# Attention and two MoE layers on one core: the first sub-chunk of the second batch multiplied in float32 itself, not in split float32r words

## The chip, the cores and the metric

The kernel runs on one core of one Trainium2 chip. The metric is the device time of one execution in microseconds (us), as the median of several runs. An instruction belongs to one of five engines: TensorE (PE, its weight loads PEld), VectorE (DVE), ScalarE (ACT), GpSimd (POOL) and SyncE (SP, which here issues nearly all DMAs). Each engine runs its own instructions in the order in which they were built; waits between engines are semaphores.

## What is computed

```python
# q, k, v: (4 batches, 8 heads, 576 positions, 64), float32
scores = q @ k^T / 8;  rel = pos_q - pos_k
scores = where((rel >= 0) & (rel < 128), scores - slope[h] * |rel|, -1e9)
x = softmax(scores) @ v                   # heads side by side: (2304, 512)
h = max(x @ w1, x @ w2, x @ w3)           # each 512 x 768
y = h @ w_out                             # 768 x 512
g, val = y @ w_gate, y @ w_val            # each 512 x 1536
out = (g * sigmoid(g) * val) @ w_out2     # 1536 x 512
```

All is float32 and has to come out close to float32. In most products the kernel splits a number into a word rounded to float32r and the rest ("high" and "low"), and adds three float32r products (high-high, high-low, low-high).

## The kernel before, in words

**Sub-chunks, pairs, units.** A batch's 576 positions are two sub-chunks (`SUBS`): s = 0 with 256 positions, s = 1 with 320. A sub-chunk has four pairs of heads p, and a pair has a unit for each block of 128 positions: two units for s = 0, three for s = 1. A unit looks at its own 128 keys and at the 128 before them; the first unit of a batch (`k0` = 128) only at its own.

**A unit** goes through four steps. `st_scores`: scores into PSUM (`sc`), the mask (L299), the bias with the row's minimum (L304), exponential on ACT. `st_normalise`: reciprocal of the sums and a scaling. `st_transpose`: two transposes into the only `pt` buffer, a copy into SBUF, and two `affine_select` on POOL that make the masked halves `t`. `st_values`: the product with v into `pv`, then `split_x` on POOL, which writes the high and low words of x.

**Two ways to multiply.** Batch 0 is `native`: `load_first` brings, for each pair, the keys of both heads as 128 rows, and a query array `q0`/`q1` in which each head's 64 rows stand beside 64 rows of zeros. One float32 product over 128 rows then gives one head's scores (L291), and values are plain float32 products (L366). All other batches are split. `load_pair` brings each head by itself (`qk0`, `qk1`: q and k side by side, written twice, on partitions 0 to 63 and 64 to 127). `prep_head` makes `r` (ACT, L256), `kl` (DVE, through the helper at L77) and the low half of `r` (POOL, L77); `prep_v` makes v's high (ACT, L265) and low words (POOL, L77). Scores are two float32r products a head (L295, L296); `st_transpose` makes a low word of the transposed weights too (DVE, L77: `t` in a first unit, `pk` otherwise); `st_values` multiplies with v's two words (L374) and adds up three parts (L378 on ACT, L379 and two L381 on DVE).

**The buffers.** `qkr` has two buffers of 128 x 832, `rv` has two. In the split way both are free as soon as the prep has read them.

**Weights.** The first layer's 18 weight tiles w_f_e come from `words` (512 KB each) and are made in `prep_w`: ACT (L90), three DVE instructions (L93, L94, L96), a rounding cast on ACT (L99), the low word on DVE (L77). `mm3` multiplies: L111 and L112 need the high word, L113 the low one.

**The order.** `spread` lays the lists of work into one another: attention of sub-chunk 0 of batch 0 with the first weights; sub-chunk 1 with the rest and with `up_groups(0, 0)` (first layer on x of sub-chunk 0, called x_329 below); the attention of batch 1, sub-chunk 0, beside `up_groups(0, 1)` (x_611) and after. `prep_next` and `load_next` run one and two pairs ahead. A scheduler then moves instructions within each engine's list by its own forecast, so the order in which they stand is a result of the build.

Of the kernel before, what the change touches and what calls it, by code (L numbers as in the profile page):

```python
# [8 lines left out]
F32 = mybir.dt.float32  # L9
# [7 lines left out]
B, H, S, D = 4, 8, 576, 64  # L17
# [3 lines left out]
P = 128  # L21
NP = H // 2
KD = DM // P
NF1, NF2 = F1 // P, F2 // P
SUBS = ((0, 256), (256, 320))
KEY0 = (0, 128)
KEYN = (256, 512)
# [23 lines left out]
def kernel(ctx: ExitStack, tc, q0, k0, q1, k1, qk0, qk1, vv, w123, wo1, wgv, wo2, out):  # L51
# [10 lines left out]
    nc = tc.nc  # L62
# [131 lines left out]
    qkr = ea("qkr", 2)  # L194
# [16 lines left out]
    def load_first(s, p):  # L211

        nq, nk = SUBS[s][1], KEYN[s]
        c0, nkb = KEY0[s] // P, nk // P
        q = hp.tile([P, 2, nq], F32, tag=f"h{s}", name="qz", bufs=NF1)
        if s == 0:
            if p % 2 == 0:
                first["k", p] = first["k", p + 1] = qkr.tile([P, 832], F32, tag="qkr", name="kn")
                first["v", p] = first["v", p + 1] = vp.tile([P, 2, 2, 2, P], F32, tag="v", name="vn", bufs=3)
            k, v = first["k", p][:, p % 2 * nk:], first["v", p][:, p % 2, 0]  # L220
        else:
            k = prep.tile([P, 832], F32, tag="r", name="kn")
            if p % 2:
                v = vp.tile([P, 4, P], F32, tag="rv", name="vn")
            else:
                v = vp.tile([P, 4, 2, P], F32, tag="v", name="vn", bufs=3)[:, :, 0]
        nc.sync.dma_start(out=k[:, :nk], in_=(k0, k1)[s][p])
        nc.sync.dma_start(out=q, in_=(q0, q1)[s][p])
        if s == 0 and p % 2 == 0:
            nc.sync.dma_start(out=first["v", p][:, :, 0], in_=vv[0, p:p + 2, :, c0:c0 + nkb].rearrange("b p k d -> p b k d"))  # L230
        elif s:
            nc.sync.dma_start(out=v[:, :nkb], in_=vv[0, p, :, c0:c0 + nkb])
        return [q, k], v

    def load_pair(b, s, p):
        n = SUBS[s][1] + KEYN[s]
        c0, nkb = KEY0[s] // P, KEYN[s] // P
        heads = []
        for a in range(2):
            raw = qkr.tile([P, 832], F32, tag="qkr", name="qkr")  # L240
            nc.sync.dma_start(out=raw[:, :n], in_=(qk0, qk1)[s][b, 2 * p + a])
            heads.append(raw)
        v = vp.tile([P, 4, P], F32, tag="rv", name="rv")
        nc.sync.dma_start(out=v[:, :nkb, :], in_=vv[b, p, :, c0:c0 + nkb, :])
        return heads, v

    def native(b):


        return b == 0  # L250

    def prep_head(s, raw):
        nq, nk = SUBS[s][1], KEYN[s]
        r = prep.tile([P, 832], F32R, tag="r", name="r")
        kl = prep.tile([P, 512], F32R, tag="kl", name="kl")
        nc.scalar.copy(r[:, :nq + nk], raw[:, :nq + nk])  # L256
        low(nc.vector, kl[:, :nk], raw[:, nq:nq + nk], r[:, nq:nq + nk])
        low(nc.gpsimd, r[D:P, :nq], raw[D:P, :nq], r[D:P, :nq])
        return r, kl

    def prep_v(s, rv):
        nkb = KEYN[s] // P
        v = vp.tile([P, 4, 2, P], F32R, tag="v", name="v", bufs=3)
        rvv = rv.rearrange("p k (a d) -> p k a d", a=2)
        nc.scalar.copy(v[:, :nkb, :, 0:D], rvv[:, :nkb])  # L265
        low(nc.gpsimd, v[:, :nkb, :, D:P], rvv[:, :nkb], v[:, :nkb, :, 0:D])
        return v
# [11 lines left out]
    pairs = {}  # L279

    def st_scores(u):
        nq = SUBS[u.s][1]
        sc = ps_s.tile([P, 2, 256], F32, tag="sc", name="sc")
        c0 = nq + u.kb * P + u.k0
        c1 = nq + u.kb * P + 256
        m = u.mq
        for a in range(2):
            o = sc[:m, a, u.k0:]
            if native(u.b):
                qz, kn = pairs[u.b, u.s, u.p][:2]  # L290
                nc.tensor.matmul(o, qz[:, a, u.q0:u.q0 + m], kn[:, c0 - nq:c1 - nq], start=True, stop=True)  # L291
                continue
            r, kl = pairs[u.b, u.s, u.p][a]
            q = r[:, u.q0:u.q0 + m]
            nc.tensor.matmul(o, q, r[:, c0:c1], start=True, stop=False)  # L295
            nc.tensor.matmul(o, q, kl[:, c0 - nq:c1 - nq], start=False, stop=True)  # L296

        own = sc[:m, :, P:]
        nc.vector.copy_predicated(out=own, mask=later[:m], data=fill[:m].to_broadcast([m, 2, P]) if u.k0 else sc[:m, :, :P])  # L299
        z = u.z = zp.tile([P, 2, P], F32, tag="z", name="z")  # L300
        mn = small.tile([P, 2], F32, tag="mn", name="mn")
        sm = u.sm = small.tile([P, 2], F32, tag="sm", name="sm")
        for a in range(2):
            nc.vector.tensor_tensor_reduce(  # L304
                out=z[:m, a], in0=own[:, a], in1=bias[:m, 2 * u.p + a],
                op0=ALU.add, op1=ALU.min, scale=-0.125, scalar=3.0e38, accum_out=mn[:m, a:a + 1],
            )
        for a in range(2):
            nc.scalar.activation(  # L309
                out=z[:m, a], in_=z[:m, a], func=AF.Exp, scale=-1.0,  # L310
                bias=mn[:m, a:a + 1], accum_out=sm[:m, a:a + 1],
            )
# [16 lines left out]
    def st_transpose(u):  # L329

        m = u.mq
        plain = native(u.b)
        n, dt = (1, F32) if plain else (2, F32R)
        pt = ps_t.tile([P, 2, P], F32, tag="pt", name="pt")
        for a in range(2):
            nc.tensor.transpose(pt[:, a, :m], u.z[:m, a], ident[:m, :m])  # L336
        if u.k0 and not plain:
            t = u.t = ptp.tile([P, 2, 2, 2, P], F32R, tag="t", name="t")
            nc.scalar.copy(t[:, 1, 0, :, :m], pt[:, :, :m])
            low(nc.vector, t[:, 1, 1, :, :m], pt[:, :, :m], t[:, 1, 0, :, :m])  # L340
            return
        if u.k0:
            t = u.t = ptp.tile([P, 2, 2, 2, P], F32, tag="t", name="tn")
            nc.scalar.copy(t[:, 1, 0, :, :m], pt[:, :, :m])
            return
        w = ptp.tile([P, 2, 2, P], F32, tag="pk", name="pk")
        t = u.t = ptp.tile([P, 2, 2, 2, P], dt, tag="t", name="t")
        nc.scalar.copy(w[:, 0, :, :m].bitcast(dt), pt[:, :, :m])
        if not plain:
            low(nc.vector, w[:, 1, :, :m], pt[:, :, :m], w[:, 0, :, :m])  # L350
        for i, (op, sign) in enumerate(((ALU.is_gt, 1), (ALU.is_ge, -1))):
            nc.gpsimd.affine_select(  # L352
                out=t[:, i, :n, :, :m], in_=w[:, :n, :, :m], compare_op=op, fill=0.0, base=0,
                pattern=[[0, n], [0, 2], [-sign, m]], channel_multiplier=sign,
            )

    def st_values(u):
        m = u.mq
        i0 = u.k0 // P
        v = pairs[u.b, u.s, u.p][2]  # L360
        pv = ps_v.tile([P, 2, 2, P], F32, tag="pv", name="pv")
        xr = small.tile([P, P], F32, tag="xr", name="xr")
        if native(u.b):
            for a in range(2):
                for i in range(i0, 2):
                    nc.tensor.matmul(  # L366
                        pv[a * D:a * D + D, 0, 0, :m], v[:, u.kb + i, a * D:a * D + D], u.t[:, i, 0, a, :m],
                        start=i == i0, stop=i == 1,
                    )
            nc.scalar.copy(xr[:, :m], pv[:, 0, 0, :m])  # L370
            return split_x(u, xr)
        for a in range(2):
            for i in range(i0, 2):
                nc.tensor.matmul(  # L374
                    pv[:, a, :, :m], v[:, u.kb + i, a, :], u.t[:, i, :, a, :m], start=i == i0, stop=i == 1
                )
        c = small.tile([D, 2, P], F32, tag="c", name="c")
        nc.scalar.copy(c[:, :, :m], pv[D:P, :, 0, :m])  # L378
        nc.vector.tensor_tensor(out=c[:, :, :m], in0=pv[0:D, :, 1, :m], in1=c[:, :, :m], op=ALU.add)  # L379
        for a in range(2):  # L380
            nc.vector.tensor_tensor(  # L381
                out=xr[a * D:a * D + D, :m], in0=pv[0:D, a, 0, :m], in1=c[:, a, :m], op=ALU.add
            )
        split_x(u, xr)
# [24 lines left out]
    def prep_next(i):  # L409
        if i < len(todo):  # L410
            heads, rv = raws.pop(todo[i])
            b, s, p = todo[i]
            pairs[b, s, p] = heads if native(b) else [prep_head(s, r) for r in heads]
            pairs[b, s, p].append(rv if native(b) else prep_v(s, rv))

    def begin():

# [15 lines left out]
    for t in range(len(units) + LV):  # L433
        if t >= LV:
            u = units[t - LV]
# [7 lines left out]
        if t < len(units):  # L443
            u = units[t]
# [208 lines left out]
```

## Time and profile before

| | us |
|---|---|
| median of 3 runs (lowest, highest) | 912.55 (912.53, 913.21) |
| the profiled execution, its own time | 910.81 |
| its span, from the first to the last instruction | 909.1 |

| engine | PE | PEld | DVE | ACT | POOL |
|---|---|---|---|---|---|
| busy us | 879.1 | 783.6 | 490.9 | 353.0 | 414.1 |
| share of the span | 97% | 86% | 54% | 39% | 46% |

The page cuts the span into 40 slices of 22.7 us. In the first five the busy digit of DVE is 7, 8, 9, 9, 8 and that of PE 8, 8, 9, 6, 8; from the sixth slice on PE is at 9 in nearly all. A share of busy time is an average over stages with different limits, so the views below are taken by stretches of the span. The spans of matmuls overlap and their ends are modelled; DVE and ACT instructions in a row overlap by a little too (some 0.08 us).

### The profile page before, as it was taken

Reading aid. Unit: us, or ns where it says so; the run is one execution under the profiler, and the core shown is the slowest. Engines: PE = TensorE matmul, PEld = TensorE weight load, DVE = VectorE, ACT = ScalarE, POOL = GpSimd, SP = SyncE. Lnnn points to the kernel's source line nnn. Section 1 sums busy time; section 2 is a strip of 40 time slices with the busy share of each in tenths; the row PEclk is TensorE's granted clock in tenths of the full one; section 3 lists DMA queues with packets and bytes.
Section 4 is the critical chain, followed back from the end, with each engine's and each line's share of the span. In section 5 each row is a group of like instructions: output and inputs, shape, how many; then the busy total and the mean of one; then the engine's idle time right before and its main releaser. Section 6 shows DMA issues by size and latency. Waiting matters only on the chain.

```text
span 909.1 us, 14915 instructions
## 1 busy us (share of the span) xinstructions
PE 879.1 (97%) x5256; PEld 783.6 (86%) x5256; DVE 490.9 (54%) x1373; ACT 353.0 (39%) x988; POOL 414.1 (46%) x599
## 2 busy tenths in 40 slices
PE   8896899999999999999998999999999999999998
PEld 6675899999999999999976788888888888888897
DVE  7899987867677686647989941111111111111121
ACT  6887647756576566513444411000010001000101
POOL 5897557676777677542325522222222122221222
PEclk9997899999999999999998999999999999999999
DMA  9755224324232430125655533000210002000100
GB/s 334 256 151 168 86 70 122 115 73 141 67 111 59 131 109 28 44 83 174 220 203 170 182 93 123 17 1 0 93 47 1 1 1 93 1 1 0 47 1 23
DMA packets 40873, 82.74 MB, mean 91 GB/s; under 512 B 3680, under 2 KB 16480, under 8 KB 40800
## 3 DMA queue, kind: packets, MB, share of 16 engines
q1 hardware_dynamic: 39712, 79.71, 27.2%
q10 hardware_dynamic: 1088, 2.10, 0.7%
q8 instruction: 41, 0.67, 0.3%
q14 instruction: 32, 0.26, 0.1%
HBM read 67.63 MB, written 14.16 MB: 90 GB/s over the span
## 4 chain that ended last, share of the span: by engine, by line
PE 75%; issue 8%; DVE 7%; POOL 6%; DMA 2%; ACT 1%; ACTq 0%; SPq 0%; POOLq 0%; DVEq 0%
PE pg L113 9%; PE pg L111 9%; PE pg L112 9%; PE ps L111 9%; PE ps L112 9%; PE ps L113 9%; PE po L533 5%; PE po L531 5%; PE po L532 5%; PE pv L374 3%; POOL a L80 2%; PE pt L336 2%; DVE wf L94 1%; POOL a L77 1%; PE sc L296 1%
## 5 line engine op out<-in xcount | busy, mean ns | idle before, releaser
L80 POOL TENSOR_SCALAR a<-sg 128x512 fp32r<-128x512 f32 (+1 forms) x60 | 48.6, 810 | 330.7 <-DVE sg L518 327.3
L111 PE MATMUL pg<-y,u 128*128 128x512 f32 (+1 forms) x480 | 176.9, 369 | 1.2 <-DVE y L77 1.2
L113 PE MATMUL pg<-y,u 128*128 128x512 f32 (+1 forms) x480 | 176.8, 368 | 0.0
L112 PE MATMUL pg<-y,u 128*128 128x512 f32 (+1 forms) x480 | 176.8, 368 | 0.0
L111 PE MATMUL ps<-x,w 128*128 128x320 f32 (+1 forms) x576 | 173.3, 304 | 2.7 <-POOL x L80 1.5
L113 PE MATMUL ps<-x,w 128*128 128x256 f32 (+1 forms) x576 | 174.4, 304 | 1.3 <-DVE w L77 1.3
L112 PE MATMUL ps<-x,w 128*128 128x320 f32 (+1 forms) x576 | 173.6, 302 | 0.0
L517 DVE TENSOR_TENSOR sg<-pg,sg 128x512 f32<-128x512 f32 (+1 forms) x60 | 38.2, 637 | 249.7 <-ACT sg L516 249.7
L516 ACT ACTIVATE sg<-pg 128x512 f32<-128x512 f32 (+1 forms) x60 | 33.4, 556 | 317.2 <-PE pg L113 313.7
L111 PEld LDWEIGHTS ps<-x,w 128*128 128x128 f32 x576 | 110.5, 193 | 5.1 <-POOL x L80 2.1
L113 PEld LDWEIGHTS ps<-x,w 128*128 128x128 f32 x576 | 110.9, 193 | 3.3 <-DVE w L77 2.3
L112 PEld LDWEIGHTS ps<-x,w 128*128 128x128 f32 x576 | 110.9, 193 | 0.5 <-POOL x L80 0.2
L111 PEld LDWEIGHTS pg<-y,u 128*128 128x128 f32 x480 | 90.8, 189 | 17.0 <-DVE y L77 1.6
L112 PEld LDWEIGHTS pg<-y,u 128*128 128x128 f32 x480 | 90.6, 189 | 15.6
L113 PEld LDWEIGHTS pg<-y,u 128*128 128x128 f32 x480 | 90.6, 189 | 15.1
L352 POOL TENSOR_SCALAR_AFFINE_SELECT t<-pk 128x512 fp32r<-128x512 f32 (+3 forms) x128 | 72.9, 592 | 42.6 <-PE pv L374 20.5
L531 PE MATMUL po<-u,a 128*128 128x512 f32 x216 | 85.1, 394 | 2.2 <-POOL a L80 2.2
L533 PE MATMUL po<-u,a 128*128 128x512 f32 x216 | 84.9, 395 | 2.3 <-POOL a L77 2.3
L532 PE MATMUL po<-u,a 128*128 128x512 f32 x216 | 84.9, 393 | 0.0
L309 ACT ACTIVATE z<-z,mn 128x128 f32<-128x128 f32 (+1 forms) x160 | 63.4, 398 | 30.9 <-DVE mn L304 29.6
L77 POOL TENSOR_TENSOR a<-sg,a 128x512 fp32r<-128x512 f32 (+1 forms) x60 | 73.1, 1218 | 5.0
L518 DVE TENSOR_TENSOR sg<-pg,sg 128x512 f32<-128x512 f32 (+1 forms) x60 | 38.2, 637 | 58.5 <-PE pg L113 58.3
(83 smaller groups left out, 1707.5 us busy)
## 6 DMA issues: line engine op xcount, KB each, us to landing
wr<-wgv SPq DMA_DIRECT2D x24, 512.0 KB, 4.2
qkr<-qk SPq DMA_DIRECT2D x24, 416.0 KB, 3.5
wr<-w SPq DMA_DIRECT2D x18, 512.0 KB, 5.5
qkr<-qk SPq DMA_DIRECT2D x24, 256.0 KB, 2.8
wr<-wo SPq DMA_DIRECT2D x12, 512.0 KB, 4.7
y<-y_dram SPq DMA_DIRECT2D x12, 512.0 KB, 5.0
y_dram<-y SPq DMA_DIRECT2D x16, 320.0 KB, 2.6
out<-ob SPq DMA_DIRECT2D x18, 256.0 KB, 2.0
```

Source lines behind the costliest of these rows:

```text
L77: eng.tensor_tensor(out=out, in0=raw, in1=head.bitcast(F32), op=ALU.subtract)
L80: nc.gpsimd.tensor_scalar(out=out, in0=in_, scalar1=1.0, scalar2=1.0, op0=ALU.mult, op1=ALU.mult)
L111: nc.tensor.matmul(ps, wh, xt_h, start=first, stop=False)
L112: nc.tensor.matmul(ps, wh, xt_l, start=False, stop=False)
L113: nc.tensor.matmul(ps, wl, xt_h, start=False, stop=last)
L309: nc.scalar.activation(out=z[:m, a], in_=z[:m, a], func=AF.Exp, scale=-1.0, bias=mn[:m, a:a + 1], accum_out=sm[:m, a:a + 1],)
L352: nc.gpsimd.affine_select(out=t[:, i, :n, :, :m], in_=w[:, :n, :, :m], compare_op=op, fill=0.0, base=0, pattern=[[0, n], [0, 2], [-sign, m ...
L517: nc.vector.tensor_tensor(out=sg, in0=pair[0], in1=sg, op=ALU.mult)
L518: nc.vector.tensor_tensor(out=sg, in0=pair[1], in1=sg, op=ALU.mult)
L531: nc.tensor.matmul(po, ah, w2[f, 2][:, 0, :], start=f == 0, stop=False)
L532: nc.tensor.matmul(po, ah, w2[f, 2][:, 1, :], start=False, stop=False)
L533: nc.tensor.matmul(po, al, w2[f, 2][:, 0, :], start=False, stop=f == NF2 - 1)
```

## The change

Batch 1, sub-chunk 0 becomes `native` as well: 4 pairs, 8 units. The test takes (b, s), and the host lays out `q0` and `k0` for two batches.

```diff
+        if native(b, s):
+            raw = qkr.tile([P, 832], F32, tag="qkr", name="qkn")
+            nq, nk = SUBS[s][1], KEYN[s]
+            q, k = raw[:, :2 * nq].rearrange("p (a n) -> p a n", a=2), raw[:, 2 * nq:2 * nq + nk]
+            nc.sync.dma_start(out=k, in_=(k0, k1)[s][b, p])
+            nc.sync.dma_start(out=q, in_=(q0, q1)[s][b, p])
+            heads = [q, k]
-        for a in range(2):
+        for a in range(0 if heads else 2):
...
-    def native(b):
-        return b == 0
+    def native(b, s):
+        return b == 0 or (b, s) == (1, 0)
...
-            pairs[b, s, p] = heads if native(b) else [prep_head(s, r) for r in heads]
-            pairs[b, s, p].append(rv if native(b) else prep_v(s, rv))
+            pairs[b, s, p] = heads if native(b, s) else [prep_head(s, r) for r in heads]
+            pairs[b, s, p].append(rv if native(b, s) else prep_v(s, rv))
```

A pair now takes one `qkr` buffer in place of two, and holds it until its last scores; its `rv` buffer is held until its last values. With the lines moved, L295/L296 read L302/L303 in the new program, L291 reads L298, L366 reads L373, L374 reads L381, L299 reads L306, L304 reads L311, L316 and L318 read L323 and L325, L336 reads L343; L77 to L120 stay. A load of `load_pair` reads L243, L244 (keys, queries), L248 (a split head) and L251 (v).

**PE, where the fifth of six weight groups is multiplied** (`sc` scores, `pt` transposes, `pv` values, `ps` the layer's sums). Before:

```order
L295 MATMUL sc<-r 128x128
L296 MATMUL sc<-kl,r 128x128
L295 MATMUL sc<-r 128x128
L296 MATMUL sc<-kl,r 128x128
L111 MATMUL ps_1283<-x_329,w_4_2_1177 128x256
L112 MATMUL ps_1283<-x_329,w_4_2_1177 128x256
L336 MATMUL pt<-ident,z 128x128 x2
L374 MATMUL pv<-t,v 128x256 x2
L113 MATMUL ps_1283<-x_329,w_4_2_1177 128x256
```

Now:

```order
L298 MATMUL sc<-qkn 128x128 x2
L373 MATMUL pv<-tn,rv 64x128 x2
L343 MATMUL pt<-ident,z 128x128 x2
L111 MATMUL ps_1252<-x_329,w_4_2_1162 128x256
L112 MATMUL ps_1252<-x_329,w_4_2_1162 128x256
L298 MATMUL sc<-qkn 128x256 x2
L373 MATMUL pv<-t,rv 64x128 x4
L113 MATMUL ps_1252<-x_329,w_4_2_1162 128x256
```

At the same weight tile the new order has attention about one unit further on: the scores of the sub-chunk's last unit stand here, which stood after w_5_0's first products before.

**DVE, at the weights w_5_1**, the last but one of the first layer. Before:

```order
L77 TENSOR_TENSOR kl<-qkr,r 128x512
L96 SCALAR_TENSOR_TENSOR wr<-wr,wf 128x512
L77 TENSOR_TENSOR kl<-qkr,r 128x512
L77 TENSOR_TENSOR t<-pt,t 128x256
L77 TENSOR_TENSOR w_5_1_1302<-wr,w_5_1_1302 128x512
L93 TENSOR_SCALAR wf<-wf 128x256
L299 COPY_PREDICATED sc<-later,sc 128x2x128
L379 TENSOR_TENSOR c<-pv,c 64x256
```

Now:

```order
L94 SCALAR_TENSOR_TENSOR wf<-wr,wf 128x512
L77 TENSOR_TENSOR kl<-qkr,r 128x512
L325 RECIPROCAL rc<-sm 128x2
L96 SCALAR_TENSOR_TENSOR wr<-wr,wf 128x512
L77 TENSOR_TENSOR kl<-qkr,r 128x512
L77 TENSOR_TENSOR w_5_1_1271<-wr,w_5_1_1271 128x512
L93 TENSOR_SCALAR wf<-wf 128x256
L306 COPY_PREDICATED sc<-later,sc 128x2x128 x2
```

`t` (the low word of the transposed weights) and `c` (the adding up of values) are gone; the `kl` that remain are of the next sub-chunk, which is split still.

**SP, the loads around the last of the first layer's weights** (w123). Before:

```order
L241 DMA qkr_1408<-qk0 128x512
L241 DMA qkr_1410<-qk0 128x512
L120 DMA wr_1300<-w123 128x1024
L244 DMA rv_1220<-vv 128x256
L241 DMA qkr_1680<-qk1 128x832
L241 DMA qkr_1682<-qk1 128x832
L120 DMA wr_1367<-w123 128x1024
L244 DMA rv_1412<-vv 128x256
L244 DMA rv_1684<-vv 128x512
```

Now:

```order
L120 DMA wr_1269<-w123 128x1024
L120 DMA wr_1333<-w123 128x1024
L243 DMA qkn_1359<-k0 128x256
L244 DMA qkn_1359<-q0 128x512
L251 DMA rv_926<-vv 128x256
L248 DMA qkr_1607<-qk1 128x832
L248 DMA qkr_1609<-qk1 128x832
L251 DMA rv_1189<-vv 128x256
```

The last two w123 loads stand ahead of the last pair's loads. The two heads of the next sub-chunk (qkr_1607, qkr_1609) stand behind a v load and wait for PE's scores out of the same two buffers; their buffers waited for DVE's and POOL's prep before.

## Rows read from the trace of the kernel before

**Rows 1.** Busy time by stretch: length, then each engine (instructions), PEclk, DMA share, GB/s

```profile
40.00:102.00 62.00, 49.12 (x335) 40.77 (x334) 59.28 (x169) 49.59 (x156) 51.52 (x73) 0.86 0.46 138
...
55.00:102.00 47.00, 34.27 (x229) 29.52 (x229) 45.32 (x124) 36.34 (x111) 37.90 (x52) 0.82 0.47 140
102.00:105.60 3.60, 3.60 (x16) 3.60 (x15) 3.56 (x17) 1.67 (x7) 0.97 (x2) 0.53 0.52 179
105.60:400.00 294.40, 293.98 (x2261) 290.03 (x2261) 215.70 (x764) 178.90 (x564) 196.79 (x335) 1.00 0.28 86
```

**Rows 2.** What PE waited for, 0 to 105 us: total us, times, longest

```profile
PE pt L336 <- DVE t L77: 6.2, 2, 3.3
```

**Rows 3.** DVE by form, 40 to 102 us: busy us, mean ns | idle before

```profile
L94 DVE SCALAR_TENSOR_TENSOR wf<-wr,wf 128x512 int32<-128x512 int32 x12 | 10.3, 860 | 0.0
L96 DVE SCALAR_TENSOR_TENSOR wr<-wr,wf 128x512 int32<-128x512 int32 x12 | 9.6, 799 | 0.0
L77 DVE TENSOR_TENSOR w<-wr,w 128x512 fp32r<-128x512 f32 x12 | 9.1, 757 | 0.0
...
L304 DVE CUSTOM_DVE_ANT_0 z<-sc,bias 128x128 f32<-128x128 f32 x22 | 5.4, 280 | 1.6 <-PE pt L336 1.6
L77 DVE TENSOR_TENSOR kl<-qkr,r 128x512 fp32r<-128x512 f32 x4 | 4.3, 1064 | 0.0
...
L77 DVE TENSOR_TENSOR kl<-qkr,r 128x256 fp32r<-128x256 f32 x6 | 3.3, 561 | 0.0
...
L77 DVE TENSOR_TENSOR t<-pt,t 128x256 fp32r<-128x256 f32 x2 | 0.8, 409 | 0.0
L381 DVE TENSOR_TENSOR xr<-pv,c 64x128 f32<-64x128 f32 x2 | 0.6, 279 | 0.0
...
L77 DVE TENSOR_TENSOR pk<-pt,pk 128x256 f32<-128x256 f32 x1 | 0.4, 416 | 0.0
L379 DVE TENSOR_TENSOR c<-pv,c 64x256 f32<-64x256 f32 x1 | 0.4, 405 | 0.0
```

**Rows 4.** DVE in order of time: start, length, instruction

```profile
56.25 0.68 DVE L94 SCALAR_TENSOR_TENSOR wf<-wr,wf 128x512 int32<-128x512 int32 x1
...
67.90 1.22 DVE L94 SCALAR_TENSOR_TENSOR wf<-wr,wf 128x512 int32<-128x512 int32 x1
```

**Rows 5.** POOL in order of time, the same place

```profile
66.87 1.70 POOL L77 TENSOR_TENSOR r<-qkr,r 64x256 fp32r<-64x256 f32 x2
```

**Rows 6.** POOL by form, 40 to 102 us

```profile
L77 POOL TENSOR_TENSOR r<-qkr,r 64x256 fp32r<-64x256 f32 x7 | 6.0, 869 | 0.3
...
L77 POOL TENSOR_TENSOR v<-rv,v 128x256 fp32r<-128x256 f32 x4 | 4.1, 1025 | 0.0
```

**Rows 7.** PE in order of time: native scores and values of a unit, then split ones

```profile
47.93 1.03 PE L291 MATMUL sc<-kn,qz 128*128 128x256 f32 x4
49.13 0.66 PE L366 MATMUL pv<-t,vn 128*64 128x128 f32 x8
...
67.93 0.28 PE L295 MATMUL sc<-r 128*128 128x256 f32 x1
...
68.28 0.28 PE L296 MATMUL sc<-kl,r 128*128 128x256 f32 x1
...
96.43 0.71 PE L374 MATMUL pv<-t,v 128*128 128x256 f32 x4 [0.28 <-DVE xr L381]
```

**Rows 8.** DMA loads of the split way: KB each, median us from issue to landing

```profile
qkr<-qk SPq DMA_DIRECT2D x24, 416.0 KB, 3.5
...
rv<-vv SPq DMA_DIRECT2D x12, 256.0 KB, 2.7
```

**Rows 9.** Forms of the prep of s = 1, whole span: busy us, mean ns | idle before

```profile
L256 ACT CAST r<-qkr 128x832 fp32r<-128x832 f32 x24 | 20.2, 882 | 3.8 <-PE sc L296 3.5
...
L77 POOL TENSOR_TENSOR v<-rv,v 128x512 fp32r<-128x512 f32 x12 | 15.5, 1291 | 0.3
...
L265 ACT CAST v<-rv 128x512 fp32r<-128x512 f32 x12 | 7.4, 619 | 0.0
```

More of the change, by code (lines that the diff above doesn't have):

```diff
@@ L226, in load_first @@
                 v = vp.tile([P, 4, 2, P], F32, tag="v", name="vn", bufs=3)[:, :, 0]
-        nc.sync.dma_start(out=k[:, :nk], in_=(k0, k1)[s][p])
-        nc.sync.dma_start(out=q, in_=(q0, q1)[s][p])
+        nc.sync.dma_start(out=k[:, :nk], in_=(k0, k1)[s][0, p])
+        nc.sync.dma_start(out=q, in_=(q0, q1)[s][0, p])
         if s == 0 and p % 2 == 0:
@@ L288, in st_scores @@
             o = sc[:m, a, u.k0:]
-            if native(u.b):
+            if native(u.b, u.s):
                 qz, kn = pairs[u.b, u.s, u.p][:2]
@@ L331, in st_transpose @@
         m = u.mq
-        plain = native(u.b)
+        plain = native(u.b, u.s)
         n, dt = (1, F32) if plain else (2, F32R)
@@ L362, in st_values @@
         xr = small.tile([P, P], F32, tag="xr", name="xr")
-        if native(u.b):
+        if native(u.b, u.s):
             for a in range(2):
@@ L615, in apart @@
     def apart(x):
-        x = x[0].reshape(NP, 2, D, -1)
-        out = np.zeros((NP, 2, D, 2, x.shape[-1]), x.dtype)
+        x = x.reshape(-1, NP, 2, D, x.shape[-1])
+        out = np.zeros((len(x), NP, 2, D, 2, x.shape[-1]), x.dtype)
         for a in range(2):
-            out[:, a, :, a] = x[:, a]
-        return out.reshape(NP, P, 2, -1)
+            out[:, :, a, :, a] = x[:, :, a]
+        return out.reshape(len(x), NP, P, 2, -1)
     arrays = {
-        "q0": apart(qt[..., 0:256]),
-        "k0": c(kt[0, ..., 0:256].reshape(NP, P, 256)),
-        "q1": apart(qt[..., 256:576]),
-        "k1": c(kt[0, ..., 128:640].reshape(NP, P, 512)),
+        "q0": apart(qt[:2, ..., 0:256]),
+        "k0": c(kt[:2, ..., 0:256].reshape(2, NP, P, 256)),
+        "q1": apart(qt[:1, ..., 256:576]),
+        "k1": c(kt[:1, ..., 128:640].reshape(1, NP, P, 512)),
         "qk0": twice(np.concatenate([qt[..., 0:256], kt[..., 0:256]], axis=-1)),
```

## The prediction, made before the changed kernel ran

> **What bounds the kernel now.** I read the busy time by stretches first. From 105.6 to 400 us PE is busy 293.98 of 294.40 us at full clock: there the time is PE's work and nothing else. From 55 to 102 us it is otherwise: PE is busy 34.27 of 47.00 us, so 12.7 us idle, while DVE is busy 45.32 [rows 1]. What PE waited for, read next, names DVE as the largest releaser: two transposes waited 6.2 us for the low word `t`, because the only `pt` buffer is free only once DVE has read it [rows 2]. The forms on DVE then show what it does there: the four instructions of each weight tile, the attention units, and the `kl`, `t`, `pk`, `c` and `xr` of the split way. The one idle time among them is 1.6 us [rows 3]. So up to 102 us the kernel is bounded by DVE, and from there by PE. A gain has to come from the moment (call it M) at which PE reaches the first product of x_611, which is at 102 us; whatever makes M earlier, or leaves PE less to do behind M, moves everything that follows, since no stage behind it hangs on anything but the work before it.
>
> **The change, part by part.** The prep of 4 pairs goes: 8 `kl`, 8 low words of q on POOL, 4 of v on POOL, 12 casts on ACT. In the 8 units the low words `t`, `pk`, one `c` and two `xr` each go.
>
> *DVE up to M.* By the built order, what has left DVE ahead of M is: 8 `kl` of 256 columns, of which 6 lie in the stretch (3.3 us; the first two lie before 40 us, where DVE soon waits, and are counted at nothing), one of the 4 `kl` of 512 (1.06), two `t` (0.8), one `pk` (0.4), one `c` (0.4), two `xr` (0.6) [rows 3]. That is 6.5 us. What has come in ahead of M, because the order moved up: one more low word of a weight (0.76) and one more unit's two reductions (2 x 0.28) [rows 3], which I round up to 2.0 for that unit's reads, sum and reciprocal. Net: **-4.5**. The units of the sub-chunk that lie behind M lose their DVE work too, at no gain: PE is the bound there and covers it.
>
> *DVE beside POOL.* The same L94 on 512 columns takes 0.68 us at 56.25 and 1.22 us at 67.90 [rows 4]. At 67.90 POOL is in the middle of two low words of q, 66.87 to 68.57 [rows 5]; the L94 ended 0.55 us after them. So a DVE instruction can stand still while POOL works. Against 0.68 us the four 512-wide forms of the stretch lost 12 x (0.860 - 0.68) + 12 x (0.799 - 0.68) + 12 x (0.757 - 0.68) + 4 x (1.064 - 0.68) = 6.0 us [rows 3]. The change takes 6.0 + 4.1 = 10.1 us [rows 6] out of POOL's 51.5 us in the stretch [rows 1], a fifth. A fifth of 6.0 is 1.2; as other forms stretch too, I take **-2.0**, with ends 0 (other POOL work closes up into the room) and -10.1 (each removed POOL instruction had held DVE for its whole length). The Trainium skill, "SBUF — State Buffer", section "Who interferes with whom", says that a DVE instruction with two SBUF inputs contends with a GpSimd instruction that reads SBUF, and that the loser blocks until the other has ended. The 67.90 row agrees; by that rule alone this term would be at its far end and the sum below -15.8 in place of -7.7, which is the third rival.
>
> *PE.* A native unit's scores take 1.03 us for four records, a split unit's run from 67.93 to 68.56, 0.63 us: 0.4 more. The values are alike: 0.66 native, 0.71 split [rows 7]. The scores of a pair's first unit, on half the columns, I take as equal. Four such units make 4 x 0.4 = 1.6 us; all lie ahead of M in the new order and find 12.7 us of idle PE [rows 1]: **0**, and +1.6 if that cover is gone.
>
> *Work taken ahead of M.* In the new order ten products of x_329, four transposes, four products of scores and a unit's values stand ahead of the first x_611 that stood behind it before. A record of this size follows the last by 0.12 us (67.93, 68.28: three steps of 0.117) [rows 7], so about 20 of them are 2.4 us that PE no longer has to do behind M. PE must find that time ahead of M, from the same 12.7 us; it also waits in order there, so I take half: **-1.2** (ends 0 and -2.4). The granted clock was 0.82 in the stretch and 0.53 from 102 to 105.6, about half speed just as PE became the bound [rows 1]; 3.6 us at half speed cost 1.7. PE was idle before it; if its stalls go, the clock may stay up: I take half, **-0.8** (ends 0 and -1.7).
>
> *The loads.* A pair's two DMAs carry less than before. But the buffers are held longer. The two heads of the next sub-chunk now wait on SP for PE's scores out of the same buffers; they waited for prep, far ahead. Behind the last native scores there come the load, 3.5 us [rows 8], the cast on ACT, 0.88 [rows 9], and `kl` on DVE, 1.06 [rows 3]: 5.4 us until the second head can be multiplied. In between PE has about 30 records at 0.12, 3.8 us. Nothing else on SP suffers at once: the last two w123 loads stand ahead, and queued behind are only heads, v and w_out pieces. What waits is DVE (its `kl` stands ahead of w_5_1) and then PE. DVE has about 20 instructions of its own in between, so I take half of the missing 1.6: **+0.8** (ends 0 and +5.4). The v loads of the next sub-chunk wait likewise for native values, behind M, with some 10 us of PE work between: 0.
>
> The sum: -4.5 - 2.0 + 0 - 1.2 - 0.8 + 0.8 = -7.7 us against the profiled execution's own time of 910.81, that is 903.1. The median of the runs shown stands at 912.55, 1.74 above it; carried over, the forecast is **904.8 us**. With the ends of single terms together (-4.5 - 4.0 - 2.4 - 1.7) it goes to about 900, and with -4.5 + 1.6 and nothing else to 909.6.
>
> **The rivals.**
>
> *PE becomes the bound of the stretch.* DVE shrinks, but PE's products stand in a fixed order among waits for weights, transposes and POOL, and the float32 scores take 1.6 us more. If half of the 12.7 us idle stays, M comes 6.35 - 1.6 = 4.7 us earlier: 907.8. For it: the clock of 0.82 makes PE slow just there. Against: its longest waits were for DVE [rows 2].
>
> *Slower: the buffers of one pair.* Held until the scores and values, they turn loads that were far ahead into loads in the chain. If the heads of both the next pairs come bare (2 x 5.4) and one v load too (2.7 + 0.62 + 1.29 = 4.6) [rows 8, 9], PE and DVE stand 15.4 us. Without the +0.8 the gains are 8.5; so +6.9: 919.5. It decides from stalls of 8.5 us on. For it: the order on SP, and only two buffers. Against: 3.8 us of PE work and some 8 us of DVE work lie in between.
>
> *POOL had held DVE by the whole.* The mechanism of the 67.90 row for all 11 removed instructions: 10.1 in place of 2.0, so 8.1 us more: 896.7. The Trainium skill, by the rule cited above, would have it so. For it: that row. Against: POOL was busy 51.5 of 62 us and yet the four forms lost only 6.0 us in all.
>
> *No change in the time.* The next sub-chunk's prep, or the changed order further on, takes the time again before PE's long stretch begins: 912.5. Against: PE has nothing to wait for from 105.6 to 400 us.
>
> **How the numbers follow.** The forecast 0.60, PE as the bound 0.20, POOL by the whole 0.07, the buffers 0.07, no change 0.06. What a measurement of this kernel tells from no change is about 0.2%, 1.8 us. Faster by more than that are the forecast, the first and the third rival: 0.87; within it 0.06; slower 0.07. The range from 899.5 to 910.0 holds the forecast with its ends and the first rival, 0.80, and leaves out the other three.
>
> **What would show it.** Right: the first product of x_611 at 93 to 96 us instead of 102; no wait of a transpose for `t` before it; DVE still the busiest there, with shorter 512-wide forms; PE's busy time up by 1 to 2 us for the scores; the stretch behind M as dense as before. Wrong: a wait of DVE's `kl` or ACT's cast for a DMA ahead of w_5_1, PE waits of 3 us or more at the next sub-chunk's first scores or values, or M earlier while the end is not.

## The result, and the profile after

The changed kernel takes **904.35 us** (median of 4 runs, 903.22 to 905.86) against 912.88 (912.53 to 913.42) for the kernel before beside it: ratio 0.9906, 95% interval 0.9888 to 0.9924. The forecast was 904.8 in 899.5 to 910.0. Two later sessions, each beside the kernel before on the same chip, gave 0.9934 (0.9911 to 0.9958) and 0.9938 (0.9918 to 0.9957), so by the medians of the three sessions the gain is between 4.6 and 8.5 us, and the agreement to half a microsecond was closer than a session can tell. The profiled execution took 905.38 us (span 903.7) against 910.81: 5.4 us less.

Busy time by stretch in the changed kernel, to be read against [rows 1]; 94.3 us is where M now lies:

```profile
40.00:94.30 54.30, 47.02 (x353) 38.59 (x353) 52.28 (x170) 45.62 (x152) 41.64 (x60) 0.96 0.44 130
55.00:94.30 39.30, 32.95 (x249) 27.33 (x247) 38.73 (x123) 33.21 (x109) 29.81 (x41) 0.94 0.47 139
94.30:105.60 11.30, 11.30 (x74) 11.29 (x74) 9.30 (x29) 7.23 (x25) 4.59 (x10) 0.89 0.35 109
105.60:400.00 294.40, 294.40 (x2246) 286.97 (x2246) 200.70 (x717) 171.82 (x540) 193.41 (x332) 1.00 0.29 89
```

M, the first product on 320 columns, in PE's order of time, in the kernel before and then in the change:

```profile
101.76 0.31 PE L111 MATMUL ps<-x,w 128*128 128x320 f32 x1
```

```profile
94.30 0.47 PE L111 MATMUL ps<-x,w 128*128 128x320 f32 x1
```

What PE waited for up to 105 us in the change (total us, times, longest); the 6.2 us of [rows 2] for `t` are gone:

```profile
PE ps L113 <- DVE w L77: 3.2, 4, 1.5
PE sc L302 <- POOL r L77: 2.4, 1, 2.4
...
PE ps L111 <- POOL x L80: 1.5, 1, 1.5
```

DVE's forms from 40 to 94.3 us in the change, as in [rows 3]:

```profile
L77 DVE TENSOR_TENSOR w<-wr,w 128x512 fp32r<-128x512 f32 x13 | 10.2, 783 | 0.0
L96 DVE SCALAR_TENSOR_TENSOR wr<-wr,wf 128x512 int32<-128x512 int32 x12 | 10.0, 834 | 0.0
L94 DVE SCALAR_TENSOR_TENSOR wf<-wr,wf 128x512 int32<-128x512 int32 x12 | 8.7, 722 | 0.0
...
L77 DVE TENSOR_TENSOR kl<-qkr,r 128x512 fp32r<-128x512 f32 x3 | 2.9, 974 | 0.0
L323 DVE TENSOR_SCALAR sm<-sm 128x2 f32<-128x2 f32 x12 | 2.8, 232 | 0.0
```

So far the forecast's picture holds: DVE is still nearly full (38.73 of 39.30 us from 55 us to M), PE's idle time there fell from 12.7 us to 6.35, and M came 7.5 us earlier. DVE's busy time between 40 us and M fell from 59.28 us [rows 1] to 52.28, by 7.0 us. But of the 7.5 us the end kept only 5.4, although from 105.6 to 400 us PE shows no idle time at all. To see where the rest went, I took every record of PE from 12 us to the first gate product (`pg<-y,u`, at 452.09 us before and 447.98 after) and split that length into three: idle (no record under way), the price of the half-speed clock (half of the busy time that lies in stretches at 1.2 GHz), and PE's work, which is the rest. The busy time is in the first column behind the length, in the kernel before and then in the change:

```profile
12.00:452.09 440.09, 421.78 (x3124) 402.16 (x3123) 343.35 (x1117) 273.70 (x846) 289.96 (x468) 0.98 0.39 123
```

```profile
12.00:447.98 435.98, 422.78 (x3144) 399.34 (x3143) 326.02 (x1077) 268.33 (x833) 279.85 (x454) 0.99 0.39 124
```

| us | length | work | idle | half clock |
|---|---|---|---|---|
| before | 440.1 | 412.6 | 18.3 | 9.2 |
| change | 436.0 | 420.0 | 13.2 | 2.8 |
| change, last session (f1_change) | 436.7 | 420.3 | 11.7 | 4.8 |

Idle and half clock together fell by 11.5 us; PE's work rose by **7.4**. At the first gate product the change leads by 4.1 us; the other 1.3 us of the 5.4 come behind it, where the profile of the change has 1.0 us less idle and 1.2 us less half clock. Where the work rose is in PE's order of time behind M. In the kernel before, the split values stand among the other products (a product of 320 columns follows the last by 0.147 us):

```profile
126.96 0.31 PE L112 MATMUL ps<-x,w 128*128 128x320 f32 x1
127.10 0.28 PE L374 MATMUL pv<-t,v 128*128 128x256 f32 x1
127.22 0.31 PE L113 MATMUL ps<-x,w 128*128 128x320 f32 x1
127.36 0.52 PE L374 MATMUL pv<-t,v 128*128 128x256 f32 x3
127.73 0.38 PE L336 MATMUL pt<-ident,z 128*128 128x128 f32 x2
```

In the change the float32 values stand there, on 64 columns of weights (128*64):

```profile
124.37 0.31 PE L112 MATMUL ps<-x,w 128*128 128x320 f32 x1
124.61 0.43 PE L373 MATMUL pv<-tn,rv 128*64 128x128 f32 x2
124.97 0.41 PE L113 MATMUL ps<-x,w 128*128 128x320 f32 x1
125.31 0.43 PE L373 MATMUL pv<-tn,rv 128*64 128x128 f32 x2
125.67 0.41 PE L111 MATMUL ps<-x,w 128*128 128x320 f32 x1
125.93 0.30 PE L112 MATMUL ps<-x,w 128*128 128x320 f32 x1
```

Before, three records take 127.73 - 127.36 = 0.37 us, 0.12 each. In the change a run of two records (one float32 product shows as two) takes 124.97 - 124.37 - 0.147 = 0.45 us, the next two 125.67 - 124.97 - 0.147 = 0.55, with a gap on either side of the run (124.61 where 124.52 would do, 125.31 where 125.12 would). The gap behind a run is 125.93 - 125.67 - 0.147 = 0.10 us; with it a run of two costs 0.56. Behind M stand 32 of the 48 value records of the sub-chunk, in 12 runs: nine of two, two of four, one of six.

### The profile page after: what moved, and what is told of

Its sections match the earlier page's. It is cut to its first block, busy times and chain, and to the rows that moved or that the text cites. A ratio compares the mean times of both kernels' runs of the same rounds, so it can differ in the third digit from the quotient of the medians.

```text
span 903.7 us, 14864 instructions
## 1 busy us (share of the span) xinstructions
PE 879.6 (97%) x5280; PEld 779.8 (86%) x5280; DVE 470.9 (52%) x1333; ACT 347.5 (38%) x976; POOL 404.1 (45%) x587
## 4 chain that ended last, share of the span: by engine, by line
PE 82%; issue 6%; DVE 5%; POOL 5%; DMA 1%; ACT 1%; ACTq 0%; SPq 0%; DVEq 0%; POOLq 0%
PE pg L111 10%; PE pg L113 10%; PE pg L112 10%; PE ps L111 10%; PE ps L113 10%; PE ps L112 9%; PE po L540 5%; PE po L538 5%; PE po L539 5%; PE pv L381 2%; PE pt L343 2%; POOL a L80 1%; PE sc L303 1%; PE sc L302 1%; DVE wf L94 1%
## 5 line engine op out<-in xcount | busy, mean ns | idle before, releaser
L113 PE MATMUL ps<-x,w 128*128 128x256 f32 (+1 forms) x576 | 173.9, 303 | 3.2 <-DVE w L77 3.2
L111 PE MATMUL ps<-x,w 128*128 128x256 f32 (+1 forms) x576 | 173.4, 303 | 1.5 <-POOL x L80 1.5
L112 PE MATMUL ps<-x,w 128*128 128x256 f32 (+1 forms) x576 | 172.5, 300 | 0.0
L77 POOL TENSOR_TENSOR a<-sg,a 128x512 fp32r<-128x512 f32 (+1 forms) x60 | 72.7, 1211 | 5.0
L316 ACT ACTIVATE z<-z,mn 128x128 f32<-128x128 f32 (+1 forms) x160 | 63.3, 398 | 22.5 <-DVE mn L311 21.9
```

Of the source, the lines that this page charges most:

```text
L77: eng.tensor_tensor(out=out, in0=raw, in1=head.bitcast(F32), op=ALU.subtract)
L111: nc.tensor.matmul(ps, wh, xt_h, start=first, stop=False)
L112: nc.tensor.matmul(ps, wh, xt_l, start=False, stop=False)
L113: nc.tensor.matmul(ps, wl, xt_h, start=False, stop=last)
L316: nc.scalar.activation(out=z[:m, a], in_=z[:m, a], func=AF.Exp, scale=-1.0, bias=mn[:m, a:a + 1], accum_out=sm[:m, a:a + 1],)
```

## The experiments

My theory at this point: M comes earlier because DVE's prep ahead of it is gone; behind M some 4.5 us are given back, because each run of values on 64 columns costs PE some 0.3 us beyond its streaming, and no idle time shows it. The rivals: what is given back comes of the order; or float32 by itself is dear; or POOL, not DVE, had set M.

**e1_grouped, f2_grouped: the values of a unit behind one another**

```diff
+            with tc.high_priority(20000 if u.b else 0):
                 for a in range(2):
                     for i in range(i0, 2):
                         nc.tensor.matmul(
...
```

> The values of batch 1, sub-chunk 0 get a high priority, so that the two or four products of a unit stand behind one another on PE; nothing else is edited. Theory (each run of float32 values among float32r products costs PE some 0.3 us beyond its streaming, which no idle time shows): 32 records behind M stand in some 6 runs in place of 12 and cost about 4 us in place of 6.96; the time falls by 2 to 3.5 us, to 901 - 902.5. Rival 1 (what is given back behind M comes from the changed order of the products or from late work, not from the switch): within 1 us of 904.35. Rival 2 (a float32 record is dear by itself, whoever stands beside it): the cost per record stays at 0.22 us, 904 - 905.

Measured: 901.85 us, ratio to the kernel before 0.9861 (0.9838 to 0.9884). It was run once more beside the change:

> As e1_grouped. Theory (2.7 us of PE's work behind M were the price of standing singly): 0.3% below the changed kernel beside it, 0.1 to 0.5. Rival (the earlier 0.45% came from the chip and the throttle of that hour): within 0.1%.

Measured: 903.13, ratio 0.9904 (0.9881 to 0.9927) where the change beside it had 0.9938: 0.34% less, as the theory has it, though the intervals overlap. PE's order of time in e1_grouped:

```profile
105.31 0.31 PE L113 MATMUL ps<-x,w 128*128 128x320 f32 x1
105.55 0.66 PE L374 MATMUL pv<-t,rv 128*64 128x128 f32 x8
106.15 0.42 PE L111 MATMUL ps<-x,w 128*128 128x320 f32 x1
106.40 0.31 PE L112 MATMUL ps<-x,w 128*128 128x320 f32 x1
...
109.18 0.31 PE L113 MATMUL ps<-x,w 128*128 128x320 f32 x1
109.42 0.44 PE L374 MATMUL pv<-tn,rv 128*64 128x128 f32 x4
109.79 0.41 PE L111 MATMUL ps<-x,w 128*128 128x320 f32 x1
```

Four records take 0.46 us, eight 0.69: the time of a run, without the 0.10 behind it, goes 0.45, 0.46, 0.69 for 2, 4 and 8 records, so most of it is paid per run. The cost per record falls to 0.09 in the run of eight, which speaks against rival 2 of the expectation. In the change itself the runs of four and of six cost 0.78 each with the record behind them, so the count alone does not give the time. The 0.9861 of e1_grouped was measured without the change beside it.

**e2_fullcols, f3_fullcols: all 128 columns of weights**

```diff
+            wide = u.b == 1
             for a in range(2):
+                o, w = (pv[:, a, 0, :m], slice(0, P)) if wide else (pv[a * D:a * D + D, 0, 0, :m], slice(a * D, a * D + D))
                 for i in range(i0, 2):
...
+                    nc.tensor.matmul(o, v[:, u.kb + i, w], u.t[:, i, 0, a, :m], start=i == i0, stop=i == 1)
+            for a in range(2 if wide else 0):
+                h = slice(a * D, a * D + D)
+                nc.scalar.copy(xr[h, :m], pv[h, a, 0, :m])
...
```

> The native values of batch 1 take all 128 columns of v as the weights, each head into a part of its own of pv, and ACT copies the right half of each; so the float32 products keep the full array and give twice the output columns' work, of which half is thrown away. If the switch is dear because the values use 64 columns of the array: a run of two records behind M falls from 0.5 us to 0.25 - 0.3, the records take up to 0.05 us more each, the time falls by 1 to 3 us (901 - 903). If it is dear because of float32 beside float32r: runs of two stay at 0.5 or more, the time is 904 - 906. Rival 1 (order): no change, 904 - 905.

> As e2_fullcols. Theory (3.7 us of PE's work saved): 0.3 to 0.5% below the changed kernel beside it. Rival (chip and throttle): within 0.1%.

Measured: 902.82, ratio 0.9860 (0.9835 to 0.9885); then 901.91, ratio 0.9889 (0.9871 to 0.9908), 0.49% below the change beside it, whose interval lies wholly above. PE's order of time in e2_fullcols:

```profile
120.54 0.31 PE L112 MATMUL ps<-x,w 128*128 128x320 f32 x1
120.69 0.38 PE L375 MATMUL pv<-t,rv 128*128 128x128 f32 x2
120.83 0.40 PE L113 MATMUL ps<-x,w 128*128 128x320 f32 x1
121.06 0.83 PE L375 MATMUL pv<-t,rv 128*128 128x128 f32 x6
121.65 0.39 PE L111 MATMUL ps<-x,w 128*128 128x320 f32 x1
121.88 0.30 PE L112 MATMUL ps<-x,w 128*128 128x320 f32 x1
...
138.77 0.28 PE L112 MATMUL ps<-h,wo 128*128 128x256 f32 x1
138.89 1.05 PE L375 MATMUL pv<-t,rv 128*128 128x128 f32 x8
139.70 0.36 PE L113 MATMUL ps<-h,wo 128*128 128x256 f32 x1
139.90 0.28 PE L111 MATMUL ps<-h,wo 128*128 128x256 f32 x1
```

Two float32 records now take 120.83 - 120.54 - 0.147 = 0.14 us in place of 0.45. The record behind a run still starts late, by 121.06 - 120.83 - 0.147 = 0.08 us; with that two records cost 0.22 in place of 0.56. Six cost (121.65 - 121.06) + (121.88 - 121.65 - 0.147) = 0.67, and eight 0.81 + 0.08 = 0.89 (a product of 256 columns follows the last by 0.12). That is 0.11 a record in every run: the same data type, half of the output thrown away, and no price per run is left. So the 64 columns were dear in short runs, not float32. The order of cost turns with the length: a run of eight costs 0.69 + 0.10 = 0.79 us on 64 columns and 0.89 on 128. The Trainium skill, "TensorEngine Tiling (Array Packing)", section "Key Properties", says that a change of the tiling mode drains TensorE. By that rule every run on 64 columns pays on its way in and out, and the rows agree; here it was about 0.3 us for a run of two.

**e3_values_split, f4_values_split: only the scores native**

```diff
-        plain = native(u.b, u.s)
+        plain = u.b == 0
...
-        if native(u.b, u.s):
+        if u.b == 0:
...
-            pairs[b, s, p].append(rv if native(b, s) else prep_v(s, rv))
+            pairs[b, s, p].append(rv if b == 0 else prep_v(s, rv))
```

> Scores of batch 1, sub-chunk 0 stay native, its values go back to the split way (prep of v, low words t, c and xr return). Theory: DVE gets 2.2 us back ahead of M and POOL the 4 low words of v and the selections of two words, so M comes 2.2 to 4 us later than in the change (96.5 - 98.5); behind M nothing is given back (-4 to -5 against the change): in all 902 - 904.5, at or below the changed kernel. Rival 1 (what is given back behind M has nothing to do with the native values): M later and nothing won behind it, 906.5 - 908.5.

> As e3_values_split. Theory (the native values win some 2 us ahead of M and give back 3.1 us of PE's work, so the float32 scores alone carry the whole gain): within 0.2% of the changed kernel beside it. Rival (the native values do carry a gain of their own): slower than it by 0.2% or more.

Measured: 905.46, 1 us above what I expected, ratio 0.9901 (0.9881 to 0.9922); then 904.57, ratio 0.9925 (0.9908 to 0.9941), 0.13% below the change beside it. M came at 97.62 us in e3_values_split, 3.3 us later than in the first profile of the change. To compare what lies behind M I count the products `ps<-x,w` ("up products") from the start: M is the 197th in the kernel before and the 207th in the change, and the 217th lies behind M in both. From there to the first gate product the lead on the kernel before fell by 1.0 us only in e3_values_split (from 7.04 to 6.07), in the change from 9.28 to 4.11. PE's work in that stretch was 344.2 us, beside 344.4 in the kernel before and 348.9 in the change. Rival 1 falls by that: the order is much the same. At the 217th product e3_values_split was 2.2 us behind the change, and f4_values_split 1.8 us behind f1_change, with a like clock ahead of it in each of these pairs. So native values on 64 columns bring nothing that these runs can tell: they win some 2 us ahead of M and give them back behind it. The two intervals beside one another overlap.

**e4_scores_split: only the values native**

```diff
-        if native(b, s):
+        if b == 0:
...
-            if native(u.b, u.s):
+            if u.b == 0:
...
-            pairs[b, s, p] = heads if native(b, s) else [prep_head(s, r) for r in heads]
+            pairs[b, s, p] = heads if b == 0 else [prep_head(s, r) for r in heads]
```

> Values stay native, the scores of batch 1, sub-chunk 0 go back to the split way (two heads in two buffers, casts, kl and the low words of q return). Theory: seven kl (4.4 us) return to DVE ahead of M and 8 low words of q to POOL, PE saves up to 1.6 us ahead of M where it is idle anyway; M 4.4 to 7 us later than in the change (98.7 - 101.3), the late load of the next heads (2.4 us of PE) goes, and what is given back behind M stays: 907.5 - 911. If POOL holds DVE by the whole length of its instructions: the 8 low words alone (6 us) come on top, 913 or more.

Measured: 912.90, ratio 0.9985 (0.9964 to 1.0005), slower than I expected, and no longer to be told from the kernel before. The miss is M: it came at 107.52 us, 5.8 us after that of the kernel before. But ten more products of x_329 stand ahead of M here, as in the change; at the 217th up product e4_scores_split is 2.9 us late (108.99 against 106.12). DVE from 40 to 107.5 us:

```profile
L311 DVE CUSTOM_DVE_ANT_0 z<-sc,bias 128x128 f32<-128x128 f32 x28 | 7.0, 278 | 1.6 <-PE pt L343 1.6
L77 DVE TENSOR_TENSOR kl<-qkr,r 128x512 fp32r<-128x512 f32 x6 | 5.3, 880 | 0.0
...
L77 DVE TENSOR_TENSOR kl<-qkr,r 128x256 fp32r<-128x256 f32 x8 | 4.8, 607 | 0.0
```

Against [rows 3] there are 28 reductions in place of 22 and six `kl` of 512 columns in place of four: the order took three more units of the next sub-chunk ahead of M. I had costed the `kl` that come back, and not the order that comes with them. That native values on 64 columns alone bring nothing is shown. How much of it the order did, how much PE's 5.4 us of added work (below the table) and how much the clock stays open: in this profile the clock was at half speed from 28.9 to 35.7 us, in that of the kernel before not ahead of 61 us.

**e5_again, e6_pool_back, e7_dve_back: the two costs that were removed, put back one at a time**

```diff
+            if (b, s) == (1, 0):
+                q, k = heads[:2]
+                low(nc.gpsimd, put[D:], k[D:], q[D:, 0])
+                low(nc.gpsimd, put[D:], k[D:], q[D:, 1])
+                low(nc.gpsimd, put, rv[:, :2].rearrange("p k d -> p (k d)"), k)
```

These are the three of e6; e7 has two, on DVE:

```diff
+            if (b, s) == (1, 0):
+                q, k = heads[:2]
+                low(nc.vector, put, k, q[:, 0])
+                low(nc.vector, put, k, q[:, 1])
```

> The changed kernel once more, beside the next three on one chip. Both theories: ratio to the kernel before 0.989 - 0.992.

> The changed kernel, and at the prep of each pair of batch 1, sub-chunk 0 POOL subtracts three times into a scratch that nothing reads: two of 64x256 from the pair's own buffer, one of 128x256 from v. So POOL has about its 10 us back, at about the places of the low words that the change took away. Theory (POOL's work costs DVE a share of its length only): 0.5 to 2.5 us slower than the changed kernel beside it, M by as much. Rival (each POOL instruction holds DVE for its whole length): 7 to 10 us slower, M at 103 us or later. Rival 2 (POOL's work is hidden): within 0.5 us.

> The changed kernel, and at the prep of each pair of batch 1, sub-chunk 0 DVE subtracts twice 128x256 into a scratch that nothing reads, 8 in all, as the kl did. Theory (DVE's work sets M): 8 x 0.53 = 4.3 us more on DVE, M and the end 3 to 5 us later than in the changed kernel beside it. Rival (M is set by PE and its clock, DVE has become second): within 1.5 us.

Measured: the change 908.11, ratio 0.9934 (0.9911 to 0.9958), above the 0.992 that I expected at most; with POOL's work back 906.78, ratio 0.9939 (0.9916 to 0.9961); with DVE's work back 910.44, ratio 0.9977 (0.9959 to 0.9994). What was put back, by tile, in e6 and then in e7 (count, shortest, median and longest ns), a form that e6 stretched, and a wait of PE's in e6:

```profile
L77 POOL TENSOR_TENSOR put<-qkn x8: 726/1052/1907, 34.1 to 93.8; 64x256 bf16<-64x256 f32 x8
L77 POOL TENSOR_TENSOR put<-rv,qkn x4: 731/736/1168, 59.5 to 128.0; 128x256 bf16<-128x256 f32 x4
...
L324 DVE TENSOR_SCALAR sm<-sm 128x2 f32<-128x2 f32 x12 | 4.1, 338 | 0.0
...
PE pv L374 <- POOL t L360: 5.6, 4, 2.5
```

```profile
L77 DVE TENSOR_TENSOR put<-qkn x8: 397/444/622, 33.2 to 76.7; 128x256 bf16<-128x256 f32 x8
```

About 11 us of POOL's work ahead of M moved the time by 0.05%, 0.5 us, and M from 97.03 us (e5) to 99.24: the rival of 7 to 10 us is out, but 0.5 to 2.5 us and nothing cannot be told apart. Two things moved with it. Some of DVE's forms grew against e5 (`w` from 731 to 806 ns, `wf` at L94 from 721 to 780, `sm` from 243 to 338; `wr` at L96 fell from 876 to 861), some 2.6 us over the stretch. And PE waited 5.6 us for POOL's selections `t`, in e5 0.8; DVE had more idle time ahead of M (5.7 us from 40 us on, in e5 3.4).

The 8 x 0.444 = 3.6 us of DVE's work moved the time by 0.43%, 3.9 us, by the ratios, inside the 3 to 5 expected, and by 2.3 us by the medians; the two intervals just part. M moved to 102.95, by 5.9 us, which is more than the work put back. These profiles differ in their clock: before 40 us e5 lost 1.7 us to half speed, e6 and e7 nothing. Against the first profile of the change, which lost nothing there either, M is 4.9 us later in e6 and 8.6 in e7. So M follows DVE's work, and POOL's less, though three times as much was put back; the sizes are known only roughly.

**e8_both: behind one another, and on 128 columns**

> The products of a unit's values behind one another (as in e1_grouped) and on all 128 columns (as in e2_fullcols). Theory: PE's work up to the first gate product, 419.8 us in the change, 417.1 grouped and 416.1 on full columns, falls to 415 - 416.5; the time is 0.4 to 0.7% below the changed kernel beside it. Rival (the two gains are the same gain, and the order alone decides): no lower than the better of the two, 0.3 to 0.5% below.

Measured: 902.78, ratio 0.9907 (0.9884 to 0.9931), 0.27% below the change beside it, with overlapping intervals; PE's work up to the first gate product 417.4 us. A miss: the work is no lower than in e1_grouped (417.1) or e2_fullcols (416.1). The two gains are one gain, since on 128 columns a record costs 0.11 us in a run of any length, so there is no price per run left to save.

**f1_change: the change beside f2, f3 and f4**

> The changed kernel for the third time, now beside the grouped values, the full columns and the split values on one chip, since its ratio was 0.9906 once and 0.9934 once. Both theories: 0.990 - 0.994.

Measured: 906.90, ratio 0.9938 (0.9918 to 0.9957). The table gives PE's work from 12 us to the first gate product, by product, at full speed, from the records of these runs (its sums lie up to 0.3 us under those of the table further up, by the way in which gaps are shared out):

| us of PE's work | before | f1_change | f2_grouped | f3_fullcols | f4_values_split |
|---|---|---|---|---|---|
| scores `sc` | 41.96 | 43.80 | 43.94 | 43.39 | 43.63 |
| values `pv` | 36.73 | 40.01 | 37.76 | 38.39 | 37.15 |
| transposes `pt` | 15.69 | 16.40 | 15.42 | 15.86 | 16.18 |
| down `ps<-h,wo` | 78.29 | 79.85 | 79.40 | 79.24 | 78.32 |
| up `ps<-x,w` | 239.83 | 239.98 | 240.75 | 239.69 | 240.20 |
| sum | 412.50 | 420.04 | 417.27 | 416.57 | 415.48 |

The way out of a run is paid by the record behind it, so the rows `h,wo` and `pt` rise as well: put down to the values, they make 3.3 + 1.6 + 0.7 = 5.6 of the 7.5 us, and the scores 1.8. With the values split again (f4_values_split) `pv` and `h,wo` are back to within 0.5 us; `pt` is not, so its 0.7 is argued. The same sum is 418.0 in e4_scores_split (+5.4).

## Why the prediction was right, and where not

**DVE up to M (-4.5): right in kind.** DVE stayed nearly full up to M (52.28 of 54.30 us), and its busy time from 40 us to M fell by 7.0 us, where this term and the next together say 6.5. e7_dve_back moved M when DVE got work. M itself came at 94.30, 97.03 and 97.62 us in three profiled executions of the change, against 101.76 in the one profile of the kernel before; only the first lies in the forecast 93 to 96. What differs between the first and f1_change is the clock: the granted clock in the stretch before 40 us was 1.00 in the first profile and 0.88 in f1_change, with 3.3 us lost by my split, and M came 3.3 us later.

The change, first profile, then f1_change:

```profile
12.00:40.00 28.00, 24.32 (x163) 17.24 (x161) 23.68 (x92) 22.82 (x82) 23.85 (x40) 1.00 0.95 347
```

```profile
12.00:40.00 28.00, 24.35 (x141) 17.20 (x140) 21.83 (x86) 20.61 (x74) 20.75 (x37) 0.88 0.91 336
```

**DVE beside POOL (-2.0): about right.** By the forecast's own yardstick of 0.68 us, the four forms lost 13 x 0.103 + 12 x 0.154 + 12 x 0.042 + 3 x 0.294 = 4.6 us in place of 6.0; the small sums `sm` fell from 372 ns to 232, another 12 x 0.14 = 1.7. Together -3.1, half more than forecast and nearer to a share than to the whole 10.1. The row of `sm` in the kernel before, by form, 40 to 102 us:

```profile
L316 DVE TENSOR_SCALAR sm<-sm 128x2 f32<-128x2 f32 x11 | 4.1, 372 | 0.0
```

The Trainium skill's rule in "SBUF — State Buffer", "Who interferes with whom", agrees with the single instruction at 67.90 us [rows 4, 5]; the step from there to all of POOL's length, which the third rival took, e6_pool_back shows to be wrong here. The low end of the range took -4.0 for this term, though its ends were given as 0 and -10.1; no row gives the -4.0.

**Scores (0, and +1.6 if the cover is gone): right.** They cost 1.4 to 2.0 us more (table), ahead of M, where PE still idles 6.35 us.

**"The values are alike: 0.66 native, 0.71 split": this step failed.** It compared one whole unit in one run of eight records [rows 7], and went on to count the values at nothing wherever they stand. The lengths of those rows run to the end of the last record, which overlaps what follows; where PE has no idle time four split records take 4 x 0.12 = 0.47 us, and a run of eight native ones 0.79 (e1_grouped). Behind M the order breaks them further, into runs of 2, 4 and 6, PE is the bound there, and 32 of the 48 records stand there in 12 runs. PE's work from the 217th up product to the first gate product rose by 4.5 us (344.35 before, 348.89 after); with the values on 128 columns (f3_fullcols) or split again (f4_values_split) it was 344.2. The forecast said of the units behind M that they "lose their DVE work too, at no gain", and did not ask what their PE work gains.

**Late loads (+0.8): another wait came.** PE waited 2.4 us for the low word of the next sub-chunk's second head, once, in the first profile and in f1_change alike. The head's cast on ACT, POOL's work behind it and PE's wait, in the first profile:

```profile
83.47 0.89 ACT L263 CAST r<-qkr 128x832 fp32r<-128x832 f32 x1
...
85.66 1.74 POOL L359 TENSOR_SCALAR_AFFINE_SELECT t<-pk 128x256 f32<-128x256 f32 x2
87.48 2.46 POOL L77 TENSOR_TENSOR r<-qkr,r 64x320 fp32r<-64x320 f32 x2
...
88.72 0.51 PE L302 MATMUL sc<-r 128*128 128x256 f32 x2 [2.41 <-POOL r L77]
```

The cast was done at 84.36 us, but POOL began the low word only at 87.48, behind `h` (from 83.91 on) and two selections. So this wait ended with POOL's order, not with the load; the forecast's chain left the low word on POOL out. One sign that I had named for being wrong did show: ACT's cast of the head after it waited 1.31 us for its load, at 85.67 us. Whether the end would gain by a third buffer for the heads was not tried.

**Granted clock (-0.8): right for what lies behind M.** The half-speed clock cost 1.7 us between M and the 217th product before; in the change it cost 1.2 in the first profile, 1.0 in e5_again and nothing in f1_change. The larger fall of the price, from 9.2 us up to the first gate product to 2.8 and 4.8 (f1_change), lies ahead of M. How much of it moved M is not shown: half speed before 40 us did, between the two profiles above.

**The sum.** That 904.8 met 904.35 so closely is luck. In the profiled pair the stretch up to the 217th product won more than the 7.7 us of the sum (a lead of 9.3 us), and 4.5 us went into the values behind M, which the sum had at nothing; the profiled execution gained 5.4 us in place of 7.7. In the two later profiles of the change the lead there was 6.8 (e5_again) and 7.0 (f1_change).

**The rivals.** The first, PE as the bound, fits the numbers as well as the forecast does: its 907.8 lies beside the later medians of 908.11 and 906.90, its M 4.7 us earlier beside 97.03, and of the 12.7 us idle just half stayed. What speaks against its mechanism is that DVE was still nearly full up to M and that e7_dve_back moved M. It may hold in part. POOL by the whole is out (e6_pool_back). "No change" came nearest to what happened behind M, a price further on that takes the gain back, but put it ahead of PE's long stretch and at the whole gain; it lies within that stretch, in the form of the values.

**The best version** is the change with its values on 128 columns: 0.9860 and 0.9889 of the kernel before, and 0.49%, 5.0 us, below the change beside it (901.91 against 906.90), for one more ACT copy per unit. The grouped values (0.9861 and 0.9904) cannot be told from it.

## What to carry to other kernels

When an operation is made cheaper on one engine by giving another a new form, price the new form in the company in which it will stand: a run of eight and a run of two are two prices. Here two float32 records between products on 128 weight columns were cheaper on all 128 columns, with half of the output thrown away (0.22 us against 0.56), and eight were cheaper on 64 (0.79 against 0.89). And where the bound changes at a moment M, ask for each moved or replaced instruction on which side of M it stands: 16 of the 48 value records stood ahead of M, where PE had idle time, and the 32 behind it cost 4.5 us.

## What the runs showed that I had not expected

- A run of float32 products on 64 weight columns among products on 128 cost 0.56, 0.57 and 0.79 us for 2, 4 and 8 records (the four and the eight in e1_grouped), the late start of the record behind it included; on 128 columns 2, 6 and 8 cost 0.22, 0.67 and 0.89. PE shows no idle time for it; it is seen only in the starts of the neighbours.
- A DVE instruction on two columns (`sm`, 128x2) is among those that POOL's work stretched most: 372 ns before, 232 in the change, 338 with POOL's work put back.
- Executions of one program in one session (e5_again) spread from 902.53 to 909.24 us, as much as the change is worth; so I compare kernels run side by side.
